# Regrouping the first transposing loads of a two-layer SiLU block: two, two and one contraction tiles

## The chip, the core and the metric

The kernel runs on one core of one Trainium2 chip. Its time is the device time of one execution in microseconds (us); where several executions are compared, the median is meant. The engines named below are PE (the matmul engine; the profile lists its weight loads apart, as PEld), ACT (activations), DVE and POOL (vector work), and SP, whose only task here is to issue DMAs.

## What is computed

The reference is a dense layer, a SiLU and a second dense layer, all in bfloat16, with matmul sums in float32 on the chip:

```python
B, S, D, F = 1, 2048, 640, 1728
h = jnp.einsum("bsd,df->bsf", x, w1)     # x: 2048 x 640, w1: 640 x 1728
h = jax.nn.silu(h)
out = jnp.einsum("bsf,fd->bsd", h, w2)   # w2: 1728 x 640
```

## The kernel before

**Tiling.** The contraction of the first layer, D = 640, is five tiles of 128, counted by k. The hidden size F = 1728 is 13 tiles of 128 and a tail of 64. The 2048 tokens are four chunks of 512 (c = 0 to 3). The first layer makes h transposed: for one F tile and one chunk, five matmuls over k add up in one of the eight PSUM banks (128 x 512 float32), and ACT writes the SiLU of the bank to `hT`. The moving operand is `xT`, x with its contraction dimension on the partitions. x lies in memory with tokens first, so SP loads it with transposing DMAs (`turned`, line 119), each for one chunk and a range of k tiles. The second layer then multiplies `hT` with `w2s` and stores the result in sixteen blocks of 128 tokens.

**The start.** The first 512 tokens are treated apart, so that PE can begin before all of x and w1 are there. For the first eight F tiles (`FA = 8`, one per PSUM bank) the loop of line 206 runs k outermost: `k_pass(k)` makes eight matmuls, one per bank, with k tile number k of x and slab number k of w1 (128 partitions x 1024 columns, 256 KB). So pass k needs only those two pieces, waits for them in line 207, and the last pass (k = 4) hands each bank to ACT. After the five passes the remaining F tiles of chunk 0 follow (line 220), five matmuls in a row for each, which wait for two further column groups of w1 (`FG`, line 117). Chunks 1 to 3 come next (line 227), with F tiles outermost.

**The loads.** All of w1, x and w2 but one piece is issued by SP, one DMA after the other in program order. The grouping of k tiles into transposes is the list `KT` (line 129): before, tile 0 alone, then tiles 1 and 2, then 3 and 4. `first(i)` issues group i for chunk 0 and notes its semaphore for every k in it; the loop of line 168 uses the same list for chunks 1 to 3. `slab(k)` issues slab k. Slab 0 is loaded in two halves, the first of them by ACT (line 147), the second by SP, and pass 0 waits for the second half only at its fifth matmul (line 199).

**The order around the barrier.** The program begins with a barrier over all engines: each engine drains and signals, POOL collects the signals and releases them. `ahead_of_start` (line 98) moves what it emits ahead of the engine's own drain, so that those DMAs are issued before the barrier. `barrier_wait_here` (line 109) moves an engine's wait for the release to the present end of the program: for SP it stands behind all loads of the start (line 161), for PE behind pass 0 (line 209). In the order before, five pieces are ahead of the drains: on SP the transpose of tile 0, the second half of slab 0, slab 1 and the transpose of tiles 1 and 2, and on ACT the first half of slab 0. Slab 2, the transpose of tiles 3 and 4, slabs 3 and 4 and the two column groups follow behind the drain.

**The dummies.** From the moment that DVE has cleared the small tile `z`, PE runs matmuls of 128 x 256 on it (`dummies`, line 181) until the first data are there; they write a bank that is overwritten by `start=True` later.

Of the kernel before, what the change touches and what calls it, by code (L numbers as in the profile page):

```python
# [9 lines left out]
def bass_standalone__dense_activation_silu__prompt_kernel(  # L10
# [16 lines left out]
    DT = D // P  # L27
# [12 lines left out]
    with ExitStack() as es:  # L40
# [18 lines left out]
        def sem(name):  # L59
            s = es.enter_context(nc.semaphore(name))  # L60
            count[s.name if hasattr(s, "name") else name] = 0
            return [s, 0]
# [6 lines left out]
        def wait(eng, *points):  # L69
            for pt in points:  # L70
                if pt is None:
                    continue
                s, v = pt
                key = (id(eng), id(s))
                if seen.get(key, 0) < v:
                    eng.wait_ge(s[0], v)
                    seen[key] = v
# [11 lines left out]
        ET = mybir.EngineType  # L89

        def preamble(engine, opcode):
            lst = nc.main_func.blocks[0].instructions
            return next(
                i for i, ins in enumerate(lst)
                if ins.opcode == opcode and ins.engine == engine
            )

        def ahead_of_start(emit, engine):
            lst = nc.main_func.blocks[0].instructions
            n = len(lst)  # L100
            r = emit()
            lst = nc.main_func.blocks[0].instructions
            new = lst[n:]
            del lst[n:]
            at = preamble(engine, "Drain")
            lst[at:at] = new
            return r

        def barrier_wait_here(engine):
            lst = nc.main_func.blocks[0].instructions  # L110
            lst.append(lst.pop(preamble(engine, "EventSemaphore")))
# [7 lines left out]
        def turned(c, k0, k1, s):  # L119
            return tick(sp.dma_start_transpose(  # L120
                out=xT[:, k0:k1, c * SCH:(c + 1) * SCH],
                in_=xf[c * SCH:(c + 1) * SCH, k0 * P:k1 * P],
            ), s, 16)

        def load_k(eng, k):
            return load(eng, w1s[:, k, 0:FA * P], w1_v[:, k, 0:FA * P])

        ld_w1 = {}
        KT = [(0, 1), (1, 3), (3, DT)]
        s_x = [sem(f"s_x{k0}") for k0, _ in KT]  # L130
        ld_x = {}

        def first(i):
            k0, k1 = KT[i]
            pt = turned(0, k0, k1, s_x[i])
            for k in range(k0, k1):
                ld_x[k] = pt
# [4 lines left out]
        def slab(k):  # L142
            ld_k[k] = load_k(sp, k)
# [5 lines left out]
            lambda: load(sp, w1s[:, 0, FH * P:FA * P], w1_v[:, 0, FH * P:FA * P]), ET.SP)  # L149
        ahead_of_start(lambda: slab(1), ET.SP)  # L150
        ahead_of_start(lambda: first(1), ET.SP)
        slab(2)
        first(2)
        slab(3)
        slab(4)
        for a, b in FG:
            e = F if b == FT else b * P
# [10 lines left out]
        for c in range(1, NSC):  # L168
            s = sem(f"s_xc{c}")
            for k0, k1 in KT:  # L170
                ld_xc[c] = turned(c, k0, k1, s)
# [9 lines left out]
        def dummies(n):  # L181
            for _ in range(n):
                pe.matmul(ps[:, 3, 0:HB], lhsT=z[:, 0:P], rhs=z[:, :], start=True, stop=True)  # L183

        wait(pe, p_z)
        dummies(13)

        def mm(o, l, r, start, stop, shared=False):
            return pe.matmul(o, lhsT=l, rhs=r, start=start, stop=stop, skip_group_check=shared)  # L189
# [7 lines left out]
        def k_pass(k):  # L197
            for ft in range(FA):
                if k == 0 and ft == FH:
                    wait(pe, ld_k[0])  # L200
                ins = mm(ps[:, ft, :], w1s[:, k, ft * P:(ft + 1) * P], xT[:, k, 0:SCH],
                         start=(k == 0), stop=(k == DT - 1), shared=True)
                if k == DT - 1:
                    silu(hT[:, ft, 0:SCH], ps[:, ft, :], ft, tick(ins, s_pe))

        for k in range(DT):
            wait(pe, ld_x[k], ld_k[k] if k else ld_k0a)
            k_pass(k)
            if k == 0:
                barrier_wait_here(ET.PE)  # L210

        nxt = [FA]
# [170 lines left out]
```

## Time and profile before

| | us |
|---|---|
| median of five executions | 125.73 (125.31 to 125.81) |
| the profiled execution | 125.64 |
| its span, from the first recorded instruction to the last | 124.3 |

The page of the profile gives, for each engine, its busy time and share of the span, then the chain of work that ended last, followed back from the end, then the costliest groups of instructions. Some of its groups that matter here (busy time, mean duration, then idle time of the engine ahead of them and what ended it):

```profile
L189 PE MATMUL ps<-xT,w1s 128*128 128x512 bf16 (+1 forms) x275 | 59.6, 383 | 0.7 <-DMA w1s<-in_w_dram 0.4
L193 ACT ACTIVATE hT<-ps 128x512 bf16<-128x512 f32 x52 | 30.0, 607 | 26.0 <-PE ps L189 26.0
L183 PE MATMUL ps<-z 128*128 128x256 bf16 x13 | 3.0, 419 | 0.4 <-DVE z L138 0.4
```

Matmuls overlap in the array, so the 383 ns of one are longer than the distance from one to the next; the timeline shows that distance. A few of the 576 matmul records are missing. The list of DMA issues gives the median time from issue to landing by size:

```profile
w1s<-in_w_dram SPq DMA_DIRECT2D x4, 256.0 KB, 3.6
xT<-in_x_dram SPq DMA_TRANSPOSE x12, 3.9
w1s<-in_w_dram ACTq DMA_DIRECT2D x1, 128.0 KB, 2.3
w1s<-in_w_dram SPq DMA_DIRECT2D x1, 128.0 KB, 3.0
```

For a single DMA the same view can be asked with a narrow window around its issue. SP's own timeline for the first third of the execution is this (start, duration of the issuing, engine, line, what):

```profile
0.00 1.23 SPq L120 DMA_TRANSPOSE xT<-in_x_dram  x1
1.29 1.03 SPq L87 DMA_DIRECT2D w1s<-in_w_dram  x2
2.37 1.26 SPq L120 DMA_TRANSPOSE xT<-in_x_dram  x1
4.12 0.33 SPq L87 DMA_DIRECT2D w1s<-in_w_dram  x1
4.50 1.23 SPq L120 DMA_TRANSPOSE xT<-in_x_dram  x1
5.77 2.10 SPq L87 DMA_DIRECT2D w1s<-in_w_dram  x4
8.01 14.35 SPq L120 DMA_TRANSPOSE xT<-in_x_dram  x9
22.40 1.19 SPq L87 DMA_DIRECT2D w2s<-in_w_dram  x2
23.63 2.19 SPq L87 DMA_DIRECT2D w2t<-in_w_dram  x2
```

A time in this view is how long SP was busy with issuing; the data land later. Consecutive issues of one kind are merged into one line. Between 3.63 and 4.12 SP ran its drain of the barrier.

### The profile page before, as it was taken

What the parts mean: (1) busy time and instruction counts of PE and PEld (TensorE: products, weight loads), DVE (VectorE), ACT (ScalarE), POOL (GpSimd) and SP (SyncE); (2) the same over time, 40 slices, a digit from 0 to 9 for tenths busy, and PEclk for the clock granted to TensorE, in tenths of its full rate; (3) what the DMA queues carried; (4) which work ended last, traced back from release to release, by engine and by line L of the source; (5) the groups of instructions that cost most, each with busy time, mean ns of one, the idle gap of its engine ahead of it and who ended that gap; (6) DMA issues with size and microseconds to landing.
All of it is one profiled execution on the core that took longest, in us unless ns stands there. A gap on an engine that the chain in (4) does not pass through costs nothing.

```text
span 124.3 us, 1329 instructions
## 1 busy us (share of the span) xinstructions
PE 120.9 (97%) x576; PEld 55.3 (44%) x587; DVE 7.5 (6%) x12; ACT 38.1 (31%) x66; POOL 0.3 (0%) x5
## 2 busy tenths in 40 slices
PE   8998999999999999999999999999999999999993
PEld 6343444444444444444434444444434444444452
DVE  0000000000000000000002020200012120102021
ACT  0400985555555555555530101010011101010100
POOL 0000000000000000000000000000000000000000
PEclk9999999999999999999999999999999999999999
DMA  5999995999000000000000000000003368111112
GB/s 118 249 252 330 210 146 111 169 335 358 22 0 0 0 5 0 3 0 0 0 0 0 5 0 0 0 0 0 0 0 75 56 220 297 53 53 53 53 59 99
DMA packets 19285, 10.35 MB, mean 83 GB/s; under 512 B 13264, under 2 KB 18768, under 8 KB 19280
## 3 DMA queue, kind: packets, MB, share of 16 engines
q1 hardware_dynamic: 19136, 10.15, 31.8%
q10 hardware_dynamic: 144, 0.13, 0.4%
q8 instruction: 4, 0.07, 0.2%
q14 instruction: 1, 0.01, 0.0%
HBM read 4.51 MB, written 2.62 MB: 57 GB/s over the span
## 4 chain that ended last, share of the span: by engine, by line
PE 90%; SPq 4%; DMA 3%; issue 1%; ACT 0%
PE ps L189 90%; DMA w1s<-in_w_dram 3%; SPq L120 3%; SPq L87 1%; SPq L368 0%; ACT o_sb L255 0%
## 5 line engine op out<-in xcount | busy, mean ns | idle before, releaser
L189 PE MATMUL ps<-xT,w1s 128*128 128x512 bf16 (+1 forms) x275 | 59.6, 383 | 0.7 <-DMA w1s<-in_w_dram 0.4
L189 PE MATMUL ps<-w2s,hT 128*128 128x512 bf16 (+2 forms) x216 | 45.0, 366 | 0.4 <-issue 0.2
L189 PEld LDWEIGHTS ps<-xT,w1s 128*128 128x128 bf16 (+1 forms) x280 | 26.7, 100 | 33.4 <-issue 1.8
L193 ACT ACTIVATE hT<-ps 128x512 bf16<-128x512 f32 x52 | 30.0, 607 | 26.0 <-PE ps L189 26.0
L189 PEld LDWEIGHTS ps<-w2s,hT 128*128 128x128 bf16 x221 | 20.9, 98 | 24.4 <-issue 1.1
L255 ACT CAST o_sb<-ps 128x512 bf16<-128x512 f32 (+1 forms) x8 | 4.4, 546 | 42.2 <-PE ps L189 42.2
L253 DVE CAST o_sb<-ps 128x512 bf16<-128x512 f32 (+1 forms) x9 | 6.1, 677 | 100.9 <-PE ps L189 98.6
L189 PE MATMUL ps<-hT,w2s 128*128 128x512 bf16 x51 | 11.3, 379 | 0.1
L189 PEld LDWEIGHTS ps<-hT,w2s 128*128 128x128 bf16 x52 | 5.1, 97 | 6.2
L255 ACT CAST oT<-ps 128x512 bf16<-128x512 f32 x2 | 1.1, 588 | 11.0 <-PE ps L189 11.0
L183 PE MATMUL ps<-z 128*128 128x256 bf16 x13 | 3.0, 419 | 0.4 <-DVE z L138 0.4
L165 ACT ACT_TABLE_LOAD x1 | 1.3, 1283 | 4.3 <-DVEq L368 4.3
L183 PEld LDWEIGHTS ps<-z 128*128 128x128 bf16 x13 | 1.8, 146 | 1.1 <-DVE z L138 0.4
L189 PE MATMUL ps<-w2t,hTt 64*128 64x512 bf16 (+2 forms) x17 | 2.2, 366 | 0.0
L253 DVE CAST oT<-ps 128x512 bf16<-128x512 f32 x2 | 1.3, 686 | 13.7 <-PE ps L189 13.7
L193 ACT ACTIVATE hTt<-ps 128x512 bf16<-128x512 f32 x2 | 1.2, 597 | 1.1 <-PE ps L189 1.1
L189 PEld LDWEIGHTS ps<-w2t,hTt 64*128 64x128 bf16 x17 | 0.7, 94 | 1.4 <-issue 0.8
L189 PE MATMUL ps<-hTt,w2t 64*128 64x512 bf16 x4 | 0.6, 381 | 0.0
L189 PEld LDWEIGHTS ps<-hTt,w2t 64*128 64x128 bf16 x4 | 0.1, 94 | 0.4 <-issue 0.4
L165 ACT ACTIVATE warm<-warm 128x32 f32<-128x32 f32 x1 | 0.2, 230 | 0.0
L138 DVE MEMSET z<- 128x128 uint32 x1 | 0.2, 165 | 0.2 <-issue 0.2
L163 POOL MEMSET warm<- 128x32 f32 x1 | 0.1, 124 | 3.8 <-POOLq L368 3.8
(4 smaller groups left out, 0.4 us busy)
## 6 DMA issues: line engine op xcount, KB each, us to landing
out_dram<-o_sb SPq DMA_DIRECT2D x15, 160.0 KB, 1.9
w2s<-in_w_dram SPq DMA_DIRECT2D x1, 1120.0 KB, 7.6
w1s<-in_w_dram SPq DMA_DIRECT2D x4, 256.0 KB, 3.6
w2s<-in_w_dram SPq DMA_DIRECT2D x1, 960.0 KB, 9.8
w1s<-in_w_dram SPq DMA_DIRECT2D x1, 480.0 KB, 5.1
w1s<-in_w_dram SPq DMA_DIRECT2D x1, 400.0 KB, 5.8
xT<-in_x_dram SPq DMA_TRANSPOSE x12, 3.9
w2t<-in_w_dram SPq DMA_DIRECT2D x2, 80.0 KB, 8.9
```

What stands on the lines that cost most here:

```text
L87: return tick(eng.dma_start(out=out_ap, in_=in_ap), s, 16)
L120: return tick(sp.dma_start_transpose(out=xT[:, k0:k1, c * SCH:(c + 1) * SCH], in_=xf[c * SCH:(c + 1) * SCH, k0 * P:k1 * P],), s, 16)
L138: p_z = ahead_of_start(lambda: tick(dve.memset(z[:, :], 0.0), s_dve), ET.DVE)
L163: p_warm = tick(pool.memset(warm[:, :], 0.0), s_pool)
L165: act.activation(out=warm[:, :], in_=warm[:, :], func=ACT.Silu)
L183: pe.matmul(ps[:, 3, 0:HB], lhsT=z[:, 0:P], rhs=z[:, :], start=True, stop=True)
L189: return pe.matmul(o, lhsT=l, rhs=r, start=start, stop=stop, skip_group_check=shared)
L193: r = tick(act.activation(out=out_ap, in_=in_ap, func=ACT.Silu), s_act)
L253: r = tick(dve.tensor_copy(out=out_ap, in_=in_ap), s_dve)
L255: r = tick(act.copy(out=out_ap, in_=in_ap), s_act)
```

## The change

The list of groups becomes two, two and one tiles. The second transpose (now tiles 2 and 3) stays ahead of the drain, and slabs 2 and 3 are issued directly behind it, also ahead of the drain; the third transpose (now tile 4 alone) and slab 4 follow behind the drain. One dummy matmul is added, and PE's wait for the barrier's release moves from behind pass 0 to behind pass 1.

```diff
-        KT = [(0, 1), (1, 3), (3, DT)]
+        KT = [(0, 2), (2, 4), (4, DT)]
...
         ahead_of_start(lambda: slab(1), ET.SP)
         ahead_of_start(lambda: first(1), ET.SP)
-        slab(2)
+        ahead_of_start(lambda: slab(2), ET.SP)
+        ahead_of_start(lambda: slab(3), ET.SP)
         first(2)
-        slab(3)
         slab(4)
...
         wait(pe, p_z)
-        dummies(13)
+        dummies(14)
...
             k_pass(k)
-            if k == 0:
+            if k == 1:
                 barrier_wait_here(ET.PE)
```

SP's order of the loads at the start, before and after:

| place | before | after |
|---|---|---|
| 1 | x tile 0 | x tiles 0, 1 |
| 2 | slab 0, second half | slab 0, second half |
| 3 | slab 1 | slab 1 |
| 4 | x tiles 1, 2 | x tiles 2, 3 |
| 5 | drain | slab 2 |
| 6 | slab 2 | slab 3 |
| 7 | x tiles 3, 4 | drain |
| 8 | slab 3 | x tile 4 |
| 9 | slab 4 | slab 4 |
| 10, 11 | column groups of w1 | column groups of w1 |

Since chunks 1 to 3 use the same list, their transposes also become two, two and one tiles, three for each chunk as before, in the same place of SP's order.

## The prediction

> **What bounds the kernel now.** I began with the page's shares. PE is busy 97% of the 124.3 us span, and the chain that ended last runs through its matmuls for 90%:
>
> ```profile
> span 124.3 us, 1329 instructions
> PE 120.9 (97%) x576; PEld 55.3 (44%) x587; DVE 7.5 (6%) x12; ACT 38.1 (31%) x66; POOL 0.3 (0%) x5
> PE 90%; SPq 4%; DMA 3%; issue 1%; ACT 0%
> ```
>
> So a change of load order can only win or lose in the remaining tenth. Where that lies, the chain in order of time shows (start, duration, what):
>
> ```profile
> 4.50 1.23 SPq L120
> 5.73 0.04 issue
> 5.77 4.16 DMA w1s<-in_w_dram
> 9.93 0.14 issue
> 10.06 2.75 PE ps L189 x12
> 12.81 0.05 issue
> 12.86 10.74 PE ps L189 x49
> 23.60 0.05 issue
> ```
>
> The chain up to 10.06 us is SP's row of issues and then one load: slab 3 of w1, issued at 5.77, landed at 9.93. From there on PE never waits for a transfer: the chain has only matmuls and breaks of 0.05 to 0.16 us. The start is therefore what the change can move, and I read it in the timeline (start, duration, engine, line, count, idle before and releaser):
>
> ```profile
> 0.39 2.96 PE L183 MATMUL ps<-z 128*128 128x256 bf16 x13 [0.39 <-DVE z L138]
> ...
> 3.14 6.56 PE L189 MATMUL ps<-xT,w1s 128*128 128x512 bf16 x24
> 3.57 0.15 PEld L189 LDWEIGHTS ps<-xT,w1s 128*128 128x128 bf16 x1 [0.27 <-issue]
> 4.00 0.15 PEld L189 LDWEIGHTS ps<-xT,w1s 128*128 128x128 bf16 x1 [0.28 <-issue]
> ...
> 4.42 0.15 PEld L189 LDWEIGHTS ps<-xT,w1s 128*128 128x128 bf16 x1 [0.28 <-DMA w1s<-in_w_dram]
> ...
> 4.85 0.15 PEld L189 LDWEIGHTS ps<-xT,w1s 128*128 128x128 bf16 x1 [0.27 <-issue]
> 5.20 0.31 PEld L189 LDWEIGHTS ps<-xT,w1s 128*128 128x128 bf16 x2 [0.20 <-issue]
> ...
> 6.07 3.14 PEld L189 LDWEIGHTS ps<-xT,w1s 128*128 128x128 bf16 x16 [0.55 <-DMA xT<-in_x_dram]
> ...
> 10.06 6.20 PE L189 MATMUL ps<-xT,w1s 128*128 128x512 bf16 x27 [0.36 <-DMA w1s<-in_w_dram]
> ```
>
> Three things are to be seen. (1) Weight loads, one per matmul, step by 0.427 us until 4.85 and then fall to half. The warm step comes from the chain: 10.79 us from 12.86 to 23.66 for 50 matmuls (ten groups of five; 49 are recorded), 0.216 us each. I call the change of pace T; here T is about 5.1. The granted-clock column reads 1.0 even before it, so only the steps show it. (2) Pass k=1 starts at 6.07, when the second transpose lands; pass k=0 had needed 4 cold and 4 warm steps from 3.14 and was through at about 5.85, so 0.22 us stood empty. (3) Passes 1 and 2 are 16 matmuls, 3.45 us, through at 9.53; slab 3 lets pass 3 begin at 10.06, another 0.53 us. Pass 4 then begins at 10.06 + 8 x 0.216 = 11.79. Everything after that is PE at full pace, so the prediction is **where pass 4 will begin**.
>
> **The change, step by step.** I give each transfer's landing before as its start in the timeline plus the time to landing that its own line gives.
>
> *First transpose, one tile to two.* Before: 0.00 + 2.9. Issue does not grow (1.23 us for one tile, 1.26 and 1.23 for two). No two-tile transpose on an empty queue is in the trace. Low end: the extra 131 KB at the rate while transposes move (the windows 4.5 to 5.5 us show 244 and 251 GB/s) is 0.52 us, so 3.4. High end: the two-tile transposes with slabs ahead of them took 3.7 from issue. I take 3.4, since only half a slab, on ACT's queue, is ahead of this one. It cannot be under 2.9.
>
> *One more dummy.* 13 of them fill 0.39 to 3.14, 0.212 us each; the fourteenth ends at 3.35, inside the wait for the transpose. It costs nothing; if the data came at 2.9 after all, it would cost 0.2.
>
> *Pass 0.* Start 3.4 plus 0.05 (pass 1 before began 0.05 after its landing): 3.45, against 3.14. With T at 5.1 the first four matmuls are cold (3.45, 3.88, 4.31, 4.73), the fifth starts at 5.16 and four warm ones reach 6.02. A start later by 0.31 thus costs only 0.17, because fewer matmuls fall into cold time. The second half of slab 0 (issue 1.29 + 3.0 = 4.3) has 131 KB more ahead of it, so 4.8 at worst, before the fifth matmul.
>
> *Pass 1* needs no transpose of its own now, and its slab (1.91 + 3.0 = 4.9) comes by 5.4. It runs 6.02 to 7.75: the 0.22 us is gone.
>
> *Pass 2* needs the second transpose (2.37 + 3.7 = 6.1, plus 0.5 = 6.6) and slab 2. SP now issues slab 2 right behind that transpose, at about 3.7 instead of 4.12, as its drain moves behind; but 131 KB more is ahead of it. Landing before 4.12 + 2.9 = 7.0; high end 7.0 + 0.5 = 7.5; low end 7.0 - 0.4 = 6.6 if issue was the limit (the DMA share was 0.77 and 0.76 in the half microseconds from 2.0 and 3.5). I take 7.4, nearer to the queue-bound end. The matmul is due at 7.75, its weight load a few tenths earlier: the tightest step. Pass 2 runs to 9.48.
>
> *Pass 3, the wait that bounded before.* Slab 3 was issued at 5.77, behind five tiles of x and a drain. Now it is issued at about 4.1 behind four tiles. Low end: slab 2's landing plus 262 KB at the 329 GB/s of 9 to 10 us, 0.8, gives 8.2; high end: its old 4.2 from issue gives 8.3. It is due at 9.48, so 1.2 us are in hand and the 0.53 us goes. **What is late next** is the last tile of x and slab 4. SP's drain (0.37) now comes at about 4.55, the one-tile transpose is issued at about 5.0 and lands at 5.0 + 2.9 to 3.7, at most 8.7. Slab 4 keeps its place in SP's row (eight issues and the drain precede it in both kernels) and the bytes ahead of it are the same: 6.39 + 4.2 = 10.6 at worst. Due 11.20: hidden by 0.6.
>
> *Pass 4* begins at 9.48 + 1.73 = 11.20, against 11.79: **0.59 us earlier**.
>
> *What else moves.* All engines leave SP's barrier about 0.9 us later, as two slab issues of some 0.45 us now stand ahead of its drain. ACT's table load moves from 4.28 to about 5.2 and with the warm-up ends by 6.8; the first silu came at 12.2. PE's barrier wait moves behind pass 1 (7.75), long after the release. The two column groups of w1 land at 6.87 + 5.1 = 12.0 and 7.34 + 5.8 = 13.1, with unchanged bytes ahead; they are due at 12.9 and 16.2. In later chunks each triple of transposes is 2, 2, 1 tiles instead of 1, 2, 2: same count and bytes, same place in SP's row; chunk 1 ends at 12.2 + 3.8 = 16.0 and is due at 23.1. Were that cover gone, each microsecond would count in full.
>
> **The sum.** The profiled execution took 125.64 us (span 124.3, 1.3 around it). 125.64 - 0.59 = 125.05; it lay 0.09 under the median of 125.73, so the forecast on the median is 125.15.
>
> **A rule against it.** T is not the kernel's to choose. The row has T at 5.1, 4.7 us after the first dummy. The Trainium skill ("TensorE: Matmul & The Clock Gate", Part 1, What's actually happening) says that the array runs at half rate until a busy window of about 3.4 us has passed, that this window runs free of the kernel's start, and that the point of change so varies. By it T could be anywhere from 0.4 + 3.4 = 3.8 to 7.2. Before, this hardly mattered: the two DMA waits swallowed a later T up to about 6.3, since pass 3 began at 10.06 anyway. After, PE carries T in full: each microsecond of later T costs about 0.5. By the row the gain is 0.59; by the rule it runs from 0.8 (T early, then slab 2's landing limits) through 0 at T = 6.3 to -0.15 at 7.2. One execution can't tell; I stay with the row. All five runs of before lie within 0.5 us, which fits a start set by transfers.
>
> **Rivals.**
> - *Same, the late clock.* T falls at 6 or later in most runs: the removed waits are filled by cold matmuls, and the time is 125.6 to 125.9. For it: the rule; against: T = 5.1 in the row. Chance 0.25.
> - *Partly hidden, slab 2 late.* If slab 2 lands at 8.0 instead of 7.4, pass 2 starts 0.3 late, which leaves 0.3: 125.45. For it: the margin is only 0.3; against: it is issued earlier. Chance 0.12.
> - *Slower, a hole that holds the clock back.* Between the last dummy (3.35) and pass 0 (3.45, or 3.75 by the high end) PE is empty, where before the dummies ran right into pass 0. If that makes the current window count as not busy, the change comes a window later, at 5.1 + 3.4 = 8.5: pass 0 is all cold and ends at 6.9, 3.8 of pass 1 are cold, and the 20 left reach 12.9, 1.1 later than 11.79: 126.8. It decides as soon as the hole passes whatever share of a window must be busy, which the trace doesn't show. Against it: at most 0.4 of 3.4 us. Chance 0.15.
> - *The forecast*, chance 0.48.
>
> **How the numbers follow.** A measurement of this kernel tells 0.3%, 0.38 us, from no change. Faster: the forecast's 0.48, less the part of it with T a little late, plus nothing else: 0.47. Within: that part, the late clock and slab 2, 0.35. Slower: the hole, and a late clock with late transfers, 0.18. The range goes from 124.75 (T early, and slab 2 at its low end) to 125.95 (late clock, and the transpose at its high end); the hole is left out.
>
> **What would show it.** Right: pass 0 begins near 3.45, no releaser "DMA xT" near 6 and no "DMA w1s" near 10, slab 3 landed before 8.5, pass 4 at about 11.2. Wrong: pass 0 starting after 3.75, a wait of pass 2 for slab 2 near 7.7, matmul steps of 0.427 us after 5.5, or a wait on slab 4 beyond 11.2.

## The result and the profile after

The changed kernel takes 125.42 us in the median of 44 executions (124.60 to 125.97), against 125.73 us of 79 executions before (125.25 to 126.69). The ratio is 0.9965 with a 95% interval of 0.9955 to 0.9975: 0.44 us gained, between 0.31 and 0.57 (the medians alone differ by 0.31). The forecast was 125.15, a gain of 0.58. Medians and ranges here and below are of all executions, while ratios leave out those over 1.5% slower than the fastest of their kernel, which occur only in the two kernels with slab 1 on ACT's queue.

The profiled execution took 125.30 us, span 124.0. Its page and its chain (start, duration, what), cut to two pieces near its start:

```profile
PE 98%; issue 1%; ACT 0%; DVEq 0%
```

```profile
...
0.39 3.17 PE ps L183 x14
3.56 8.69 PE ps L189 x35
...
```

The chain has no DMA and no SP in it any more. It goes from the dummies straight into the passes. The timeline of the start shows the same (start, duration, engine, line, count, idle before and releaser):

```profile
3.37 12.98 PE L189 MATMUL ps<-xT,w1s 128*128 128x512 bf16 x53
...
5.49 0.15 PEld L189 LDWEIGHTS ps<-xT,w1s 128*128 128x128 bf16 x1 [0.28 <-issue]
5.83 0.10 PEld L189 LDWEIGHTS ps<-xT,w1s 128*128 128x128 bf16 x1 [0.19 <-issue]
6.10 1.55 PEld L189 LDWEIGHTS ps<-xT,w1s 128*128 128x128 bf16 x8 [0.17 <-DMA w1s<-in_w_dram]
...
11.86 4.51 ACT L193 ACTIVATE hT<-ps 128x512 bf16<-128x512 f32 x9 [5.11 <-PE ps L189]
```

Three readings. PE's matmuls are one merged row from 3.37 us on, where before the row broke at 10.06. Such a row can hide a short wait (the first row of before runs on through the wait that ended at 6.07), so the weight loads count as well: none of them waits for a DMA after 6.10. The step between weight loads still is 0.43 us at 5.49 and falls only there, so the clock changed at T = 5.7 and not at 5.1. And the weight load of pass 1 waited a little for slab 1, although no matmul did: slab 1 landed at 6.06, 0.2 us before the first matmul of pass 1 started on its step, at 6.26.

The first SiLU starts 0.416 us after the first matmul of pass 4. It stands at 11.86 now, and before it stood at 12.20:

```profile
12.20 4.03 ACT L193 ACTIVATE hT<-ps 128x512 bf16<-128x512 f32 x8 [6.40 <-PE ps L189]
```

That is 0.34 earlier, all of 125.64 - 125.30. This yardstick holds through all profiles that follow. T is read from the steps of the matmuls, which fall from 0.427 to 0.216 us. (The granted-clock column reads 1.0 ahead of T, as the prediction says, but only because the trace has no record of the clock there: in the first four kernels of the table the record begins at 5.12, 5.73, 5.46 and 5.72, which are the T of the steps; the other seven have no record at all.)

| kernel | first real matmul | T | first SiLU | profiled time | difference |
|---|---|---|---|---|---|
| before | 3.14 | 5.1 | 12.20 | 125.64 | 113.44 |
| changed | 3.37 | 5.7 | 11.86 | 125.30 | 113.44 |
| changed, again | 3.62 | 5.5 | 11.92 | 125.36 | 113.44 |
| changed, 13 dummies | 3.49 | 5.7 | 11.90 | 125.36 | 113.46 |
| slab order alone | 3.14 | 3.3 | 11.74 | 125.19 | 113.45 |
| slab order alone, again | 3.14 | 3.6 | 11.76 | 125.22 | 113.46 |
| grouping alone | 3.42 | 3.5 | 11.92 | 125.38 | 113.46 |
| changed, 9 dummies | 3.40 | 7.6 | 12.78 | 126.26 | 113.48 |
| before, no dummies | 2.92 | 8.4 | 12.93 | 126.42 | 113.49 |
| changed, no dummies | 3.55 | 6.7 | 12.41 | 125.86 | 113.45 |
| second transpose first | 3.58 | 9.8 | 14.38 | 127.86 | 113.48 |

The last column varies by 0.05 us while the times vary by 2.7; the two kernels with slab 1 on ACT's queue, left out of the table, have 113.45 and 113.46. So everything that the change and the experiments do is done before the first SiLU.

### The profile page after: what moved, and what is told of

It is laid out like the page before. It is cut to its first block, busy times and chain, and to the rows that moved or that the text cites. A ratio compares the mean times of both kernels' runs of the same rounds, so it can differ in the third digit from the quotient of the medians.

```text
span 124.0 us, 1331 instructions
## 1 busy us (share of the span) xinstructions
PE 121.0 (98%) x577; PEld 55.4 (45%) x588; DVE 7.5 (6%) x12; ACT 38.1 (31%) x66; POOL 0.3 (0%) x5
## 4 chain that ended last, share of the span: by engine, by line
PE 98%; issue 1%; ACT 0%; DVEq 0%
PE ps L189 95%; PE ps L183 3%; ACT o_sb L255 0%; DVEq L368 0%
```

## The experiments

My theory after the result: the transfers no longer hold the start, PE's own pace does, and that pace depends on a T that each execution draws anew. The rivals: the spread of times comes from transfers that land late; or only one of the two edits brings the gain.

### The changed kernel once more

No edit.

> The changed kernel once more, beside the others on one chip. Clock theory (PE sets the start now; the time T at which the matmul step falls from 0.427 to 0.216 us varies from execution to execution between about 3.8 and 7.2 us, and each microsecond of T costs 0.5): median near 125.4, spread of about 1 us between the fastest and the slowest, and in the profile the start of pass 4 at 11.2 + 0.5 x (T - 5.1), whatever T this execution has. Rival (the spread comes from transfers that land late by chance): pass 4's start goes with the landing of slab 1 or slab 2 and not with T, with a DMA as releaser ahead of it.

Measured: median 125.37 (124.81 to 125.73, 16 executions), ratio 0.9967 (0.9951 to 0.9983). This profile has T = 5.5. By the rule in the expectation its pass 4 should start at 11.4; the first SiLU at 11.92 puts it at 11.50. The other 0.1 has two sources. Pass 0 began at 3.62 instead of 3.45, worth half of that, and slab 2 landed at 7.9, so that pass 2 began at 8.05, where PE alone would have begun it at 7.97. So both kinds of delay occur, the clock with 0.2 and late transfers with 0.1 to 0.2.

The spread does not decide between them. Of all executions listed with the result, the middle 80% of the changed kernel span 1.0 us (124.71 to 125.72), those of before 0.6 (125.45 to 126.04). But the sixteen of this repeat span 0.6, as do those of the kernel before that ran beside them, and the grouping alone (below), whose pass 3 waits for a transfer, spans 0.85. How much of the spread is T's is not shown.

### The slab order alone

```diff
-        KT = [(0, 2), (2, 4), (4, DT)]
+        KT = [(0, 1), (1, 3), (3, DT)]
...
-        dummies(14)
+        dummies(13)
```

(against the changed kernel; slabs 2 and 3 stay ahead of the drain, and PE's wait for the barrier behind pass 1)

> Only slabs 2 and 3 go ahead of the third transpose (and of SP's drain); the transposes stay one, two, two tiles, 13 dummies. Theory that the slab order alone brings the gain: slab 3 lands near 8.5 instead of 9.9, pass 0 begins at 3.14, pass 1 waits for the second transpose until about 6.1 as before, the third transpose (two tiles, issued at about 5.0) lands near 9.3, just before pass 3 is due at 9.5; median 125.2 to 125.4, with less spread than the full change since pass 1 still waits at 6.1. Rival, that the regrouping is needed: the two-tile third transpose lands after 9.9 and the time stays at 125.7 or more.

Measured: 125.22 (125.00 to 125.48, 10 executions), ratio 0.9950 (0.9933 to 0.9967). The weight loads in its timeline:

```profile
3.11 0.64 PEld L189 LDWEIGHTS ps<-xT,w1s 128*128 128x128 bf16 x4 [0.25 <-DMA xT<-in_x_dram]
4.34 0.55 PEld L189 LDWEIGHTS ps<-xT,w1s 128*128 128x128 bf16 x4 [0.58 <-DMA w1s<-in_w_dram]
6.08 1.41 PEld L189 LDWEIGHTS ps<-xT,w1s 128*128 128x128 bf16 x8 [1.20 <-DMA xT<-in_x_dram]
7.75 1.47 PEld L189 LDWEIGHTS ps<-xT,w1s 128*128 128x128 bf16 x8 [0.26 <-DMA w1s<-in_w_dram]
9.58 2.92 PEld L189 LDWEIGHTS ps<-xT,w1s 128*128 128x128 bf16 x15 [0.36 <-DMA xT<-in_x_dram]
```

Here the clock was early (T = 3.3), and transfers start nearly everything: the second half of pass 0 waits for slab 0 until 4.34, pass 1 for the second transpose until 6.08, pass 3 for the third until 9.58, though that last wait moved its matmul by only 0.03 us. At 7.75 the weight load waited without holding up a matmul at all. But slab 3, which held pass 3 until 10.06 before, lands at 8.4. **The slab order alone is enough for the gain.** The same kernel once more:

> The slab order alone (one, two, two tiles) a second time, beside the changed kernel with 13 dummies: its first figures rest on 10 executions. Clock theory: it starts pass 0 some 0.3 us earlier and waits at about 6.1 for the second transpose whatever T is, so median 125.15 to 125.3 and a spread of 0.3 to 0.6, not 1.0; at or a little under the changed kernel.

Measured: 125.21 (125.04 to 125.42, 6 executions), ratio 0.9946 (0.9926 to 0.9965). The narrow spread, 0.4 to 0.5 us in both, fits a start held at 6.1 by a transfer that lands alike (6.04 and 6.11 in the two profiles). This kernel is not slower than the full change; the intervals overlap, so that it is faster is not shown.

### The grouping alone

```diff
-        KT = [(0, 1), (1, 3), (3, DT)]
+        KT = [(0, 2), (2, 4), (4, DT)]
...
-        dummies(13)
+        dummies(14)
```

(against the kernel before)

> Only the grouping two, two, one and the fourteenth dummy; slab 2 stays behind the drain and slab 3 behind the third transpose. Theory that the slab order alone brings the gain: ahead of slab 3 lie the same five tiles and three slabs as before, it lands near 9.9, pass 3 waits for it, and the time is 125.6 to 125.8. Rival, that the grouping brings the gain by taking away pass 1's wait for x: 125.3 to 125.5.

Measured: 125.66 (124.82 to 126.00, 22 executions), ratio 0.9980 (0.9965 to 0.9995). One weight-load row of its timeline tells why there is so little:

```profile
9.76 2.27 PEld L189 LDWEIGHTS ps<-xT,w1s 128*128 128x128 bf16 x12 [1.09 <-DMA w1s<-in_w_dram]
```

Pass 3 waits for slab 3 as before, until 9.76 instead of 10.03. Passes 0 to 2 were early (T = 3.5) and the time they had won was lost in this one wait, 0.8 us by the steps of the matmuls. The ratio leaves a gain of 0.06 to 0.44 us, more than I expected at its upper end; in this profile slab 3 landed 0.2 earlier than before with the same bytes ahead of it. In some executions it must have landed earlier still: the fastest, 124.82, is 0.56 under the profiled 125.38, and by the yardstick of the table its pass 3 began that much earlier, at 9.2 (an estimate; that execution has no trace). So landing times make part of the spread. PE's wait for the barrier stands behind pass 0 here, as before, and cost nothing: pass 1 began on PE's own step (5.34 to 5.55), so that its place is no part of the slab order's gain.

### A hole in PE's start

```diff
-        dummies(14)
+        dummies(9)
```

(against the changed kernel)

> The changed kernel with 9 dummies instead of 14: PE is empty from about 2.5 us to 3.4 us. If a hole of 0.9 us doesn't keep a window from counting as busy: T as ever, time as the changed kernel's, 125.3 to 125.5. If it does: T comes about 3.4 us later in the executions whose window holds the hole (some 6 in 10), the median rises by 0.5 to 1.5 us to 125.9 to 126.9, and T in the profile is likely beyond 7.2.

Measured: 126.43 (125.76 to 126.85, 10 executions), ratio 1.0048 (1.0023 to 1.0072). Its weight loads:

```profile
3.40 0.13 PEld L189 LDWEIGHTS ps<-xT,w1s 128*128 128x128 bf16 x2 [1.38 <-DMA xT<-in_x_dram]
...
7.22 0.15 PEld L189 LDWEIGHTS ps<-xT,w1s 128*128 128x128 bf16 x1 [0.28 <-issue]
7.62 4.85 PEld L189 LDWEIGHTS ps<-xT,w1s 128*128 128x128 bf16 x23 [0.25 <-issue]
```

The first transpose landed as ever, and pass 0 began at 3.40. But cold steps (those of 0.43 us) go on to 7.22: T is 7.6. No transfer held a matmul up after 3.40, so the 0.96 us between this profile and that of the changed kernel (126.26 - 125.30) is the clock's: half of the 1.9 us between the two T. This is the rival "slower" of the prediction, made to happen; the kernel becomes slower than before.

The other side of it, a smaller hole:

```diff
-        dummies(14)
+        dummies(13)
```

> The changed kernel with 13 dummies as before, not 14: PE is empty from 3.1 us to the landing of the first transpose at about 3.35 (0.2 to 0.4 us). If the fourteenth costs and brings nothing, the median is that of the changed kernel, 125.3 to 125.5. If even a hole of 0.3 us keeps windows from counting, the median rises as with 9 dummies, though less: 125.6 to 126.2.

Measured: 125.19 (124.88 to 125.36, 6 executions), ratio 0.9935 (0.9913 to 0.9957). By the step of the dummies PE was empty from 3.14 to 3.49 (the profile, which adds the tail of the last dummy, counts 0.15 as idle), and T was 5.7 all the same. The median is a little under both expectations, so a hole of this size did no harm, and that the fourteenth dummy brings anything is not shown.

### Without dummies

```diff
-        dummies(14)
+        dummies(0)
```

(and `dummies(13)` to `dummies(0)` in the kernel before)

> The kernel before without its dummy matmuls. PE starts with pass 0 at 2.9 us, so the change of pace T can come only after a busy window from there: between about 5.8 and 9.3 us, near 7.5 in the middle. Clock theory: about 10 cold matmuls instead of 4; by the chain of the profile (slab 3 still lands at 9.9) pass 4 starts between 11.8 and 12.9, median time about 126.0 (125.7 to 126.9).

> The changed kernel without its dummy matmuls. PE starts with pass 0 at 3.4 us, T between 6.2 and 9.8. Clock theory: nothing but PE's own pace is left in the start, the later first matmul counts in full, pass 4 starts near 12.5 and the median is about 126.4, that is about 0.3 to 0.5 SLOWER than the kernel before without dummies: the sign of the change turns with the clock. Rival (the gain is that of the transfers' order and doesn't depend on the clock): it stays 0.3 to 0.5 faster than the kernel before without dummies.

Measured: before without dummies 126.12 (125.51 to 126.72), ratio to the kernel before 1.0029 (1.0014 to 1.0043); changed without dummies 126.20 (125.59 to 127.17), ratio 1.0042 (1.0022 to 1.0063), 22 executions each. The gain of 0.44 us is gone. In the profile of before without dummies, T is 8.4 and no transfer holds a matmul up: slab 3 landed at 10.16, and pass 3 began on PE's own step at 10.79. In an execution with so late a clock the order of the loads had nothing to win. That the sign turns, as I expected, is not shown, since the two intervals overlap.

### Can the early clock be used?

In the slab-order kernel an early clock is wasted at the wait for the second transpose. Three tries to land it earlier. First, from SP alone, the transpose directly behind the first one:

```diff
         ahead_of_start(lambda: first(0), ET.SP)
+        ahead_of_start(lambda: first(1), ET.SP)
...
         ahead_of_start(lambda: slab(1), ET.SP)
-        ahead_of_start(lambda: first(1), ET.SP)
```

(against the slab order alone)

> As slabs_only, but the second transpose is issued directly behind the first one, ahead of the second half of slab 0 and slab 1, all on SP's queue. Theory (the start is paced by the bytes in SP's one queue): the transpose lands near 4.5 instead of 6.0, but slab 0's second half comes near 4.8 instead of 4.3 and slab 1 near 6.0 instead of 5.0, so pass 1 still starts near 6.0 and pass 2 still waits for slab 2 near 7.8: median within 0.15 of slabs_only's 125.2. Rival (SP's issue order holds pass 1 back): pass 1 starts near 5.6 and the median falls to 124.9.

Measured: 127.62 (126.14 to 127.98, 6 executions), ratio 1.0108 (1.0060 to 1.0156). Neither expectation holds. The profile is of an execution of 127.86; two of the six, at 126.1 and 126.3, lost less. The second transpose did land early, at 4.8, but the second half of slab 0 only at 6.0:

```profile
6.08 0.13 PEld L189 LDWEIGHTS ps<-xT,w1s 128*128 128x128 bf16 x2 [1.52 <-DMA w1s<-in_w_dram]
...
9.87 2.69 PEld L189 LDWEIGHTS ps<-xT,w1s 128*128 128x128 bf16 x13 [0.24 <-issue]
```

PE stood still in the middle of pass 0, and the second row shows the price: the cold steps end only there, T = 9.8. The wait itself was 0.6 us by the profile's idle column; against the slab order alone the time lost is over 2.

Second and third, slab 1 on ACT's queue instead of SP's, so that SP comes to the transpose 0.5 us sooner:

```diff
-        ahead_of_start(lambda: slab(1), ET.SP)
+        def slab_act(k):
+            wait(act, ld_k0a)
+            ld_k[k] = load_k(act, k)
+
+        ahead_of_start(lambda: slab_act(1), ET.Activation)
```

(against the slab order alone; and the same without the wait)

> As slabs_only (one, two, two tiles; slabs 2 and 3 ahead of the drain), but slab 1 is issued by ACT as soon as its half of slab 0 has landed, so that SP issues the second transpose at about 1.9 instead of 2.4. Theory (in early-clock executions pass 1 waits for the second transpose, which waits for SP): it lands near 5.5 instead of 6.0, pass 1 starts up to 0.5 earlier where the clock is early, the median falls by 0.2 to 0.4 against slabs_only to about 124.9 to 125.1, and the spread grows again to some 0.8. Rival (the transpose is limited by the bytes ahead of it, not by SP's issuing): it lands at 6.0 as before and the median stays at 125.2.

> The same without ACT's wait: slab 1 is issued at about 0.5 us. Its 256 KB then share the DMA engines with the first transpose. Theory: the first transpose lands later, at 3.2 to 3.6 instead of 2.9 to 3.1, and the second earlier, near 5.4; the first costs half of its delay (cold matmuls), so the median is between that with the wait and 0.15 above it. Rival (the extra queue costs the first transpose nothing): median as with the wait or lower.

Measured: with the wait 129.06 in the median (126.97 to 130.99, 7 executions), ratio 1.0114 (1.0078 to 1.0151) from three of the seven; without it 126.96 (124.57 to 127.74, 17 executions), ratio 0.9957 (0.9939 to 0.9976) from seven of the seventeen. The expected times fell in both. The profile with the wait is of its longest execution, 130.99, and speaks for that one alone. The second transpose (issued at 1.91) took this long to land, and PE's row is (line 193 is the matmul here):

```profile
DMA to landing us min/median/max: 7.1/7.1/7.1
```

```profile
9.06 4.45 PE L193 MATMUL ps<-xT,w1s 128*128 128x512 bf16 x10 [3.28 <-DMA xT<-in_x_dram]
```

The granted clock is the third number from the end in the row of the last stretch of waiting (0.53); over 9 to 10 us it is 0.50:

```profile
8.00:9.00 1.00, 0.00 (x0) 0.00 (x0) 0.00 (x0) 0.00 (x0) 0.00 (x0) 0.53 0.76 199
```

The second transpose landed at 9.0 instead of 6.0, slab 1 at 8.8 instead of 5.0. PE was empty for 3.3 us, and afterwards ran at half clock again: ten matmuls in 4.45 us. Without the wait it was the first transpose that landed late, at 4.5 instead of 3.1, in the profile of an execution of 125.33; ten others took 126.9 to 127.7, and none of those has a trace. Neither version is of use.

## Why the prediction was right, and what was off

**What bounds it.** Right. All of the difference lies before the first SiLU, as the table shows, and the rest of the execution is the same to 0.05 us.

**First transpose.** Taken as 3.4, measured 3.3, a little under the low end of the range given, and 3.6 in the repeat, inside it. **Dummy.** Free, as costed.

**Passes 1 to 4.** The two waits went, as forecast. The landings were later than the sum had them: slab 1 at 6.1 (forecast: by 5.4), the second transpose at 7.2 (6.6), slab 2 at 7.8 (7.4), slab 3 at 8.4 (8.2 to 8.3), the third transpose at 9.0 (at most 8.7). Only slab 4, at 10.6, was as written. In the profiled execution none of this cost anything, because the clock was late as well: with T at 5.1 pass 1 would have been due at 5.95 and slab 1, landing at 6.06, would have held it. The repeat had slab 1 at 5.4 and lost 0.1 at slab 2. So the margins that I called tight are eaten now and then.

**The later chunks.** They stayed covered, but the cover is thinner than the sum had it. Chunk 1 was not due at 23.1: behind pass 4 chunk 0 has only five more F tiles, 25 matmuls or 5.4 us, so it was due at 18.3 by the forecast, and its first matmul ran at 18.56. Its transposes had landed by 16.5.

**The term that was mis-sized** is T, taken from one execution at 5.1. It is 5.7 and 5.5 in the two profiles of the changed kernel. The prediction's own price, 0.5 us for each microsecond of T, gives 11.20 + 0.31 = 11.51 for the first; less half of the 0.08 by which pass 0 began early, 11.47; measured 11.44. So the mechanism and the price were right and the input was a single draw from a wide distribution. One of the signs of being wrong that the prediction named, steps of 0.427 us after 5.5, thus came about, by 0.2 us. The rule set against the row in the prediction (a window of about 3.4 us that runs free of the kernel's start) was the better guide to the size: it said a gain between 0.8 and -0.15 by T, and the measured mean lies inside. Its lower end for T, 3.8, was too high all the same: the profiles of the slab order alone and of the grouping alone have 3.3 to 3.6.

**The rivals.** The late clock is one end of a range and not a case beside the forecast: the three profiles of the changed kernel with 13 or 14 dummies have T at 5.5 to 5.7, between the forecast's 5.1 and the rival's 6. Slab 2 late occurs, at 0.1. The hole that holds the clock back was not seen in the profiles of the change, where the dummies left at most a small one, but the 9-dummy kernel shows that it exists. There pass 4 began 0.6 later than before, where the rival had 1.1: its T was 7.6 and not 8.5, which at half a microsecond for each makes the difference.

**What I did not see.** The sum credited the regrouping with the 0.22 us at pass 1 and charged it 0.17 for the later start, as parts of one gain. Taken alone it is worth 0.06 to 0.44 us, and the slab order alone is worth as much as both together. The wait for slab 3, behind the third transpose, was the one that had to go.

## What to carry to other kernels

When transfers set the start of a kernel, removing their waits hands the start to PE's clock, and a single profile then says little about the size of the gain: take several and read the step between matmuls in each. Keep PE filled up to the first real matmul and until the clock has changed, since a stall of under 1 us there can cost a further window of 3.4 us at half pace; after the change, stalls of 0.6 and 0.7 us in the idle column of the matmuls (the grouping and the slab order alone) left the pace as it was. Make one move at a time: here the place of two slabs in the queue carried the gain, and the regrouping added to it nothing that could be told apart.

## What the runs showed of the hardware

- The clock is judged in windows of 3.4 us here. In the profile with slab 1 on ACT's queue the steps fall at 4.65 us and the granted clock drops at 8.06 (0.53 over 8 to 9 us), 3.41 later. In the profile of before the clock's end fits the same grid: over 124 to 125 us, behind the last matmul, it reads 0.79, which puts the drop to 0.5 at 124.58, and the 119.46 us since T = 5.12 are 35 times 3.413:

```profile
124.00:125.00 1.00, 0.00 (x0) 0.00 (x0) 0.00 (x0) 0.00 (x0) 0.00 (x0) 0.79 0.00 0
```

- The window counted from T backwards tells how much idle time it may hold. The change came as early as 3.3 us, 2.9 us after the first dummy; that window began before the dummies and held about 0.5 us in which PE did nothing. Windows with about 0.9 us of empty PE did not count: with 9 dummies (0.91 idle, T = 7.6) and with the early second transpose (0.24 and 0.62 idle, T = 9.8). Where between 0.5 and 0.9 us the limit lies stays open.
- With slab 1 on ACT's queue beside the transposes on SP's, one execution had both land far later than with all on SP's queue: the second transpose took 7.1 us instead of 3.7, the 256 KB slab 6.3 instead of 3.0. That they delayed each other is not shown, and why was not tried. The half slab that ACT loads beside the first transpose in every kernel lands after 2.3 us in the profile of before, so two queues at once are not enough for it.
- Landing times of the same DMA in the same order differ between executions: slab 1 of the changed kernel at 6.1 and 5.4, its second transpose at 7.2 and 6.4.
